# A new order for batches 0 to 2 of a two-stage attention and feed-forward kernel: transposes behind more matmuls, loads and transposes in other places

## The chip, the core and the metric

The kernel runs on one core of one Trainium2 chip. The metric is the device time of one execution in microseconds, lower is better. The core's engines are TensorE (PE, with its weight loads shown as PEld), VectorE (DVE), ScalarE (ACT), GpSimd (POOL) and SyncE (SP), which here only issues DMAs. Each engine works through its own list of instructions in order and waits for others by semaphores.

## The reference

The inputs are x (8 batches, 8 heads, 512 rows, 64 columns), a state of 32 rows per batch and head, and two weights of 512x2048 and 2048x512. For every batch and head the rows of x attend to the 32 state rows, and the state rows attend to x; both results are laid one under the other (544 rows a batch), heads side by side (512 columns), and go through a leaky feed-forward layer.

```python
scores = scale * np.matmul(x, state.transpose(0, 1, 3, 2))
a = softmax(scores)                      # max taken off, exp, divided by the sum + 1e-09
xread = np.matmul(a, state)
a2 = softmax(scale * np.matmul(state, x.transpose(0, 1, 3, 2)))
sread = np.matmul(a2, x)
attn = np.concatenate([xread, sread], axis=2)
h = attn_rows @ w_in                     # attn_rows: 4352 x 512
out = np.maximum(0.01 * h, h) @ w_out    # 4352 x 512, float32
```

## The kernel before

The 8 batches are worked one after the other, each through the same steps, and the steps of neighbouring batches are interleaved so that TensorE always has matmuls to do.

For a batch, x is loaded as float32 (`load_x`, tile `xl`, one buffer, 1 MB), cast to bfloat16 (`cast_x`, tile `xb`) and transposed by a DMA that SP issues (`a_xt_dma`, L207, tile `xT`). Batches 0 and 1 are transposed on TensorE instead (`turn` for batch 1, L1095: eight 128x128 transposes into `pxt`, evicted to `xT` by VectorE). `a_scores` (L223) makes the scores `sc` from `xT` and the state. VectorE and ScalarE make two softmaxes of it: over the state rows (`a_top`, `a_rows`, `a_less`, `a_exp`, `a_probs`, result `aT`), and over x's rows (`a_max2`, `a_exp2`, result `e2`). `a_a2t` (L330) transposes `e2` by a DMA into `a2T`, which `a_sread_rows` (L357, tile `psn`, called `rows` below) reads to make the second attention's product.

xread is never made by itself: `a_m` (L391, tile `pm`; `m_make`, `mk`) multiplies state and w_in into M, which is evicted to bfloat16 (`m_take`, `ev`), and `ff1` (L412, tile `ph`; `ff(j)`, `f.j`) multiplies M and `aT`, whose leaky ReLU (`relu`, `r.j`, L418) is the hidden tile `hT`. The second layer is made in two ways. Batch 0 uses plain matmuls: `piece(0, h0, i, jq)` (L697) adds up four (or with `part` two) of the 16 products of one output tile in PSUM (`py`, or `pyw`, the wide one), and `y_store` copies and stores the tile. Batches 1 to 7 use seven products instead of eight for a 2x2 block product, cut into units of two matmuls (L768, tile `yq`; `before.run(1)`, `u`); `sums` (L757) and `weights_sum` (L734) make the operands, `done` (`d.n`) saves or joins the products and issues the stores (L807).

Each engine's order is written out by hand: `tc.manual_schedule` keeps the order in which the program text emits the instructions for each of the five engines, so one line of the text can move an instruction on TensorE, another on VectorE, and a DMA in SP's list. Batch 1's part is a list of calls (from L1118 on). From batch 2 on `stretch(b, ...)` reads a string of short names; batch 2 has its own, FIRST, and batches 3 to 6 share ORDER. In these strings `l4` and `loads` are loads of x (`loads` of batch b + 3), `casts.h` its casts on GpSimd, `turn` the DMA transpose of batch b + 2, `a2t` the transpose of this batch's `e2`, `S` the next batch's scores, `st` the second group of the state, `sb` and `sn` operand sums of the earlier and the present batch. ORDER, used for batch 3, begins `sb.0.4 qs.0 u sb.1.4 rows S`: its `rows` for batch 3 reads the `a2T` of batches 1 and 2.

SP's order before, from batch 2 of x on, was: the state's transpose, both halves of batch 2's `xT`, the load of batch 3's x, `a2T` of batch 0, three stores of batch 0, half of the state's second group, `a2T` of batch 1, `xT` of batch 3, a store, the rest of the state, the load of batch 4's x, the state's second transpose, the load of batch 5's x, `a2T` of batch 2, `xT` of batch 4, two stores of batch 1.

Of the kernel before, what the change touches and what calls it, by code (L numbers as in the profile page):

```python
# [9 lines left out]
P = 128  # L10
# [20 lines left out]
def kernel(  # L31
# [255 lines left out]
    def a_rows(a):  # L287
        a.mb = block_rows(a.m1, NB)
# [402 lines left out]
    def piece(b, hT, i, jq, bank=None, copy=SCA, part=range(4)):  # L691
        if jq == 0:
            y = ys[b, i] = Y()
            y.py = psum.tile([P, DM], FP32, name="py", tag="py")[:] if bank is None else bank
        y = ys[b, i]
        for j in (4 * jq + v for v in part):
            nc.tensor.matmul(  # L697
                y.py, lhsT=hT[:, j, P * i:P * (i + 1)], rhs=w_out_bf[:, j, :],
                start=(j == 0), stop=(j == 15),
            )  # L700
        if jq == 3 and copy is not None:
            y_store(b, i, copy)
# [83 lines left out]
    class Batch:  # L786
# [44 lines left out]
        def done(self, n, bank, copy=SCA):  # L831
            f = self.f
            if n in (1, 6, 5, 7):
                f.save(n, bank, copy)
            if n == 2:
                f.join(self.yo(0)[:, :, :HC], bank, 1)
                if self.b == B - 1:
                    self.out(0, slice(0, HC))
            elif n == 7:
                nc.gpsimd.tensor_tensor(  # L840
                    out=self.yo(1)[:, :, HC:], in0=f.sv[7][:], in1=f.sv[5][:], op=ALU.add
                )
                if self.b == B - 1:
                    self.out(1, slice(HC, DM))
            elif n == 3:
                f.join(self.yo(0)[:, :, HC:], bank, 6)
                for i in range(2) if self.b in (2, 3, 4) else (None,):
                    self.out(0, slice(HC if self.b == B - 1 else 0, DM), i)
            elif n == 4:
                f.join(self.yo(1)[:, :, :HC], bank, 7)  # L850
                self.out(1)
# [247 lines left out]
    def cast_x1(u):  # L1099
        VEC(  # L1100
            a1.xb[:, :, NK * u:NK * (u + 1)].rearrange("p t h d -> p h t d"),
            x1[u][:].rearrange("p h (t d) -> p h t d", t=NT),
        )
# [10 lines left out]

    h1 = hpool.tile([P, 16, S], BF16, name="hT", tag="hT")
    before = Batch(1, h1)
    wide = psum.tile([P, 2, DM], FP32, name="pyw", tag="big", bufs=1)
    a_exp2(a0, 0)  # L1118
    piece(0, h0, 0, 0)
    load_state(0)  # L1120
    cast_x1(0)
    turn(0)
    cast_x1(1)
    piece(0, h0, 2, 0, bank=wide[:, 0])
    piece(0, h0, 1, 0)
    a_exp2(a0, 1)
    VEC(a1.xT[:, :, 0:2, :], pt[0][:])
    turn(1)
    VEC(a1.xT[:, :, 2:4, :], pt[1][:])
    piece(0, h0, 3, 0, bank=wide[:, 1])  # L1130
    m_make(a1, 1, "ph")
    open_xb(2)
    weights_open()
    a_scores(a1)
    m_take(a1, 1, 0, SCA)
    m_take(a1, 1, 1, VEC)
    a_top(a1)
    piece(0, h0, 0, 1, copy=None, part=(0, 1))
    piece(0, h0, 1, 1, copy=None, part=(0, 1))
    piece(0, h0, 2, 1, copy=None, part=(0, 1))  # L1140
    piece(0, h0, 1, 1, copy=None, part=(2, 3))
    m_make(a1, 2, "ph")
    m_take(a1, 2, 0, SCA)
    m_take(a1, 2, 1, SCA)
    weights_sum(2, 0, 4, nc.gpsimd)
    weights_sum(0, 0, 4, nc.gpsimd)
    state_t(0)
    piece(0, h0, 0, 1, copy=None, part=(2, 3))
    piece(0, h0, 2, 1, copy=None, part=(2, 3))
    piece(0, h0, 3, 1, copy=None, part=(0, 1))  # L1150
    m_make(a1, 3, "ph")
    piece(0, h0, 2, 2, copy=None, part=(0, 1))
    piece(0, h0, 1, 2, copy=None, part=(0, 1))
    a_rows(a1)
    a_less(a1)
    a_exp(a1)
    a_max2(a1)
    cast_x(2, 0, 4, SCA)
    cast_x(2, 4, 5, POO)
    cast_x(2, 5, 6, POO)  # L1160
    cast_x(2, 6, 7, POO)
    a_open(a2, 2)
    cast_x(2, 7, 8, POO)
    a_probs(a1, 0)
    piece(0, h0, 0, 2, copy=None, part=(0, 1))
    a_xt_dma(a2, slice(1, 2))
    piece(0, h0, 0, 2, copy=None, part=(2, 3))
    piece(0, h0, 3, 1, copy=None, part=(2, 3))
    piece(0, h0, 2, 2, copy=None, part=(2, 3))
    piece(0, h0, 3, 2, copy=None, part=(0, 1))  # L1170
    a_xt_dma(a2, slice(0, 1))
    a_exp2(a1, 0)
    a_probs(a1, 1)
    piece(0, h0, 1, 2, copy=None, part=(2, 3))
    piece(0, h0, 3, 2, copy=None, part=(2, 3))
    load_x(3, nc.sync)
    open_xb(3)
    piece(0, h0, 3, 3, copy=None, part=(0, 1))
# [27 lines left out]
    relu.pop(3)()
    y_store(0, 2, SCA)
    y_store(0, 3, SCA)
    piece(0, h0, 0, 3, copy=None, part=(0, 1))
# [21 lines left out]
    relu.pop(9)()
    y_store(0, 1, VEC)
    a_exp(a2)
    a_probs(a2, 0)
    before.run(1)
    a_probs2(a0)
# [16 lines left out]
    ff(14)
    relu.pop(14)()
    ff(15)
    relu.pop(15)()
# [326 lines left out]
```

## Time and profile before

| | |
|---|---|
| time before, median of 3 runs | 201.84 us (201.51 to 201.92) |
| profiled execution, its own time | 201.93 us |
| its span, first to last instruction | 200.2 us |
| mean granted TensorE clock | 1.000 |
| busy: PE, PEld | 193.9 us (97%), 136.5 us (68%) |
| busy: DVE, ACT, POOL | 164.7, 150.5, 62.2 us |
| DMA over the span | 28.02 MB, mean 140 GB/s |
| chain of work that ended last | PE 89%, DMA 6% |

The profile is one execution. Times in its timeline count from the first instruction; a row has a start, a length, the engine, the line of the kernel, the operation, what is written and read, and how many such instructions are merged in it. A bracket gives the idle time ahead of it and who ended it. SPq rows are DMAs that SP issues: their length is the time of the issue, not of the transfer. Matmul lengths overlap, since they are pipelined; the distance between two starts is what a matmul costs.

### The profile page before, as it was taken

What the parts mean: (1) busy time and instruction counts of PE and PEld (TensorE: products, weight loads), DVE (VectorE), ACT (ScalarE), POOL (GpSimd) and SP (SyncE); (2) the same over time, 40 slices, a digit from 0 to 9 for tenths busy, and PEclk for the clock granted to TensorE, in tenths of its full rate; (3) what the DMA queues carried; (4) which work ended last, traced back from release to release, by engine and by line L of the source; (5) the groups of instructions that cost most, each with busy time, mean ns of one, the idle gap of its engine ahead of it and who ended that gap; (6) DMA issues with size and microseconds to landing.
All of it is one profiled execution on the core that took longest, in us unless ns stands there. A gap on an engine that the chain in (4) does not pass through costs nothing.

```text
span 200.2 us, 5119 instructions
## 1 busy us (share of the span) xinstructions
PE 193.9 (97%) x2090; PEld 136.5 (68%) x2090; DVE 164.7 (82%) x283; ACT 150.5 (75%) x287; POOL 62.2 (31%) x90
## 2 busy tenths in 40 slices
PE   7999899999999999999999999999999999999992
PEld 2566544345677667776777777767777788799881
DVE  2676579799998989998999899999899977995622
ACT  3478728699778749996999679987999778767610
POOL 8483266591046013310422040400040024004350
PEclk9999999999999999999999999999999999999999
DMA  6999997999543994734393613080023402210035
GB/s 201 210 207 264 238 296 128 183 282 248 146 147 70 303 285 91 228 151 115 68 246 114 177 34 72 7 258 0 3 83 127 82 0 108 105 56 0 7 98 164
DMA packets 39992, 28.02 MB, mean 140 GB/s; under 512 B 25440, under 2 KB 36832, under 8 KB 39968
## 3 DMA queue, kind: packets, MB, share of 16 engines
q1 hardware_dynamic: 34176, 20.35, 38.1%
q0 software_dynamic: 4960, 6.55, 16.1%
q10 hardware_dynamic: 832, 0.79, 1.2%
q8 instruction: 16, 0.26, 0.6%
q14 instruction: 8, 0.07, 0.1%
HBM read 17.30 MB, written 8.91 MB: 131 GB/s over the span
## 4 chain that ended last, share of the span: by engine, by line
PE 89%; DMA 6%; DVE 1%; POOL 1%; ACT 0%; issue 0%
PE yq L768 43%; PE ph L412 18%; DMA x<-in_x_dram 6%; PE pm L391 4%; PE pyw L697 4%; PE py L697 3%; PE pf L490 3%; PE pl L658 3%; PE yu L768 3%; PE pspin L143 2%; PE pl L579 2%; PE psn L357 1%; PE sc L223 1%; PE phw L425 1%; PE pxt L1095 1%; PE yz L768 0%
## 5 line engine op out<-in xcount | busy, mean ns | idle before, releaser
L418 ACT ACTIVATE hT<-ph 128x512 bf16<-128x512 f32 x84 | 48.9, 609 | 12.3 <-PE ph L412 12.1
L768 PEld LDWEIGHTS <-su 128*128 128x128 bf16 x480 | 46.2, 98 | 12.6 <-ACT hT L418 0.4
L412 PE MATMUL ph<-aT,M 128*128 128x512 bf16 x168 | 47.6, 379 | 0.0
L768 PEld LDWEIGHTS <-hT 128*128 128x128 bf16 x336 | 32.3, 98 | 11.7 <-issue 2.5
L768 PE MATMUL yq<-tw_xf,su 128*128 128x256 bf16 x224 | 30.9, 273 | 0.0
L768 PE MATMUL yq<-w_out_bf,hT 128*128 128x256 bf16 x224 | 29.2, 273 | 0.0
L840 POOL TENSOR_TENSOR yo<-sv,sv 128x512 f32<-128x512 f32 x7 | 9.3, 1329 | 42.6 <-ACT e L311 38.2
L412 PEld LDWEIGHTS <-M 128*128 128x128 bf16 x168 | 16.0, 98 | 7.9 <-issue 1.9
L757 DVE TENSOR_TENSOR su<-hT 128x1024 bf16<-128x1024 bf16 x28 | 19.0, 682 | 2.7 <-ACT hT L418 2.7
L1288 ACT CAST M<-pm 128x512 bf16<-128x512 f32 x31 | 17.3, 599 | 1.4 <-PE pm L391 1.4
L114 POOL CAST xb<-xl 128x512 bf16<-128x512 f32 (+1 forms) x24 | 13.5, 604 | 12.6 <-DMA xl<-in_x_dram 12.6
L777 ACT COPY sv<-yq 128x512 f32<-128x512 f32 x24 | 13.9, 585 | 4.1 <-PE yq L768 4.0
L768 PE MATMUL yq<-tw_x,su 128*128 128x256 bf16 x112 | 16.6, 273 | 0.0
L780 DVE TENSOR_TENSOR yo<-yq,sv 128x512 f32<-128x512 f32 x20 | 13.5, 676 | 2.2 <-PE yq L768 2.2
L768 PE MATMUL yq<-w_out_bf,su 128*128 128x256 bf16 x112 | 15.3, 273 | 0.0
L768 PE MATMUL yq<-tw_x,hT 128*128 128x256 bf16 x104 | 13.9, 273 | 0.0
L311 ACT ACTIVATE e<-sc,mcol 128x512 bf16<-128x512 f32 x16 | 11.1, 698 | 0.0
L670 ACT COPY ls<-pl 128x512 f32<-128x512 f32 x16 | 9.5, 591 | 1.6 <-PE pl L658 1.4
L697 PEld LDWEIGHTS <-hT 128*128 128x128 bf16 x64 | 5.8, 98 | 7.0 <-issue 1.1
L757 DVE TENSOR_TENSOR su<-su,hT 128x1024 bf16<-128x1024 bf16 x14 | 9.6, 687 | 0.2
L305 DVE TENSOR_REDUCE mcol<-sc 128x2 f32<-128x1024 f32 x8 | 9.7, 1215 | 0.0
L1302 POOL COPY after<-mrow 128x1 f32<-128x1 f32 x3 | 0.6, 187 | 28.9 <-DVE mrow L233 28.9
(193 smaller groups left out, 359.9 us busy)
## 6 DMA issues: line engine op xcount, KB each, us to landing
xl<-in_x_dram SPq DMA_DIRECT2D x5, 1024.0 KB, 6.4
out_dram<-yo SPq DMA_DIRECT2D x9, 512.0 KB, 2.9
out_dram<-yo SPq DMA_DIRECT2D x9, 256.0 KB, 2.7
w_in_bf<-in_moe_w_in_dram POOLq DMA_DIRECT2D x4, 512.0 KB, 8.0
w_out_bf<-in_moe_w_out_dram POOLq DMA_DIRECT2D x2, 512.0 KB, 13.5
x<-in_x_dram POOLq DMA_DIRECT2D x2, 512.0 KB, 12.1
w_out_bf<-in_moe_w_out_dram POOLq DMA_DIRECT2D x4, 256.0 KB, 12.6
xl<-in_x_dram POOLq DMA_DIRECT2D x2, 512.0 KB, 15.2
```

Source lines behind the costliest of these rows:

```text
L114: copy(xs[b][:, h0 // NK, :, h0 % NK:h0 % NK + h1 - h0].rearrange("p t h d -> p h t d"), xl[b][:, h0:h1].rearrange("p h (t d) -> p h t d", ...
L305: nc.vector.tensor_reduce(out=a.m2[:], in_=a.sc[:], axis=AX.X, op=ALU.max, negate=True)
L311: nc.scalar.activation(out=a.e2[:, g], in_=a.sc[:, g, :], func=AF.Exp, bias=a.m2[:, g:g + 1], accum_out=a.r2[:, g:g + 1],)
L412: nc.tensor.matmul(ph[:], lhsT=a.M[:, g, P * j:P * (j + 1)], rhs=a.aT[:, g, :], start=(g == 0), stop=(g == 1),)
L418: nc.scalar.activation(out=hT[:, j, :], in_=ph[:], func=AF.Prelu, scale=1.0 / SCALE, alpha=0.01)
L670: copy(self.sv[n], flat)
L697: nc.tensor.matmul(y.py, lhsT=hT[:, j, P * i:P * (i + 1)], rhs=w_out_bf[:, j, :], start=(j == 0), stop=(j == 15),)
L757: (eng or nc.vector).tensor_tensor(out=S[n][:, ms], in0=u[:, ms], in1=v[:, ms], op=op)
L768: nc.tensor.matmul(bank[:, i, :], lhsT=lhs[:, m, P * i:P * (i + 1)], rhs=rhs[:, m, :], start=(first and m == 0 and (i == 0 or of is not No ...
L777: copy(t[:], bank)
L780: nc.vector.tensor_tensor(out=dst, in0=bank, in1=self.sv[n][:], op=ALU.add)
L1288: copy(t.M[:, g, DM * c:DM * (c + 1)], src[g][:] if isinstance(src, list) else src[:, g, :])
```

## The change

Batch 1's two sets of TensorE transposes and the pieces of batch 0 around them stand in another order: two pieces go ahead of the first set instead of one. After that the order of all five engines is another one, up to the end of batch 2's stretch (the list of calls and FIRST); ORDER stays. On SP the load of batch 3's x now goes between the two halves of batch 2's `xT`; batch 1's `a2T` and the first half of the state's second group go ahead of batch 0's stores; batch 4's `xT` goes ahead of batch 1's two stores, and the load of batch 5's x and batch 2's `a2T` go behind them. Some casts, evictions and copies change their engine. Apart from this part, batch 4 stores its first half with one transfer of 512 KB instead of two of 256 KB. The matmuls are the same in number and shape.

```diff
@@ Batch.done @@
             elif n == 3:
                 f.join(self.yo(0)[:, :, HC:], bank, 6)
-                for i in range(2) if self.b in (2, 3, 4) else (None,):
+                for i in range(2) if self.b in (2, 3) else (None,):
                     self.out(0, slice(HC if self.b == B - 1 else 0, DM), i)
@@ batch 1 @@
-    wide = psum.tile([P, 2, DM], FP32, name="pyw", tag="big", bufs=1)
     a_exp2(a0, 0)
     piece(0, h0, 0, 0)
+    cast_x1(0)
     load_state(0)
-    cast_x1(0)
+    cast_x1(1)
+    wide = psum.tile([P, 2, DM], FP32, name="pyw", tag="big", bufs=1)
+    piece(0, h0, 1, 0)
     turn(0)
-    cast_x1(1)
     piece(0, h0, 2, 0, bank=wide[:, 0])
-    piece(0, h0, 1, 0)
-    a_exp2(a0, 1)
-    VEC(a1.xT[:, :, 0:2, :], pt[0][:])
     turn(1)
-    VEC(a1.xT[:, :, 2:4, :], pt[1][:])
-    piece(0, h0, 3, 0, bank=wide[:, 1])
-    m_make(a1, 1, "ph")
     open_xb(2)
     weights_open()
+    VEC(a1.xT[:, :, 0:2, :], pt[0][:])
+    weights_sum(0, 0, 4, nc.gpsimd)
+    piece(0, h0, 3, 0, bank=wide[:, 1])
+    VEC(a1.xT[:, :, 2:4, :], pt[1][:])
+    a_exp2(a0, 1)
+    weights_sum(2, 0, 4, nc.gpsimd)
+    m_make(a1, 1, "ph")
     a_scores(a1)
...
-    cast_x(2, 0, 4, SCA)
-    cast_x(2, 4, 5, POO)
-    cast_x(2, 5, 6, POO)
-    cast_x(2, 6, 7, POO)
-    a_open(a2, 2)
-    cast_x(2, 7, 8, POO)
-    a_probs(a1, 0)
-    piece(0, h0, 0, 2, copy=None, part=(0, 1))
-    a_xt_dma(a2, slice(1, 2))
-    piece(0, h0, 0, 2, copy=None, part=(2, 3))
...
-    a_xt_dma(a2, slice(0, 1))
-    a_exp2(a1, 0)
+    a_open(a2, 2)
+    a_max2(a1)
+    cast_x(2, 0, 2, POO)
+    a_probs(a1, 0)
     a_probs(a1, 1)
+    cast_x(2, 2, 4, POO)
+    m_take(a1, 3, 0, SCA)
+    cast_x(2, 4, 8, SCA)
     piece(0, h0, 1, 2, copy=None, part=(2, 3))
+    a_xt_dma(a2, slice(1, 2))
+    piece(0, h0, 0, 2, copy=None, part=(2, 3))
     piece(0, h0, 3, 2, copy=None, part=(2, 3))
     load_x(3, nc.sync)
     open_xb(3)
...
+    a_xt_dma(a2, slice(0, 1))
+    a_exp2(a1, 0)
     cast_x(3, 0, 2, POO)
     a_exp2(a1, 1)
-    m_take(a1, 3, 0, SCA)
+    a_a2t(a0)
+    load_state(1, range(0, 2))
+    a_a2t(a1)
+    m_make(a2, 0, "sc")
...
-    a_a2t(a0)
-    a_scores(a2)
+    relu.pop(3)()
+    a_top(a2)
+    y_store(0, 3, SCA)
...
     FIRST = (
-        "f.1 f.0 l4 sb.0.4 u u r.1 u r.0 u f.2 d.1.A sb.2.0 f.3 mk.3.big r.2 S d.2 u u u sb.1.4 "
-        "tp ev.3.0.A r.3 f.4 u rows sb.2.4 u rw sb.3.4 u u u casts.0 casts.2 st u u u casts.4 f.5 "
-        "u ls sb.3.0 u u x2 casts.6 loads a2t turn u u ev.3.1.A d.6.A r.4 r.5 u w3 f.6 u d.5.A "
-        "f.7 r.6 u r.7 u f.9 ex u rc f.8 u u u u r.8 u r.9 u f.11 u u d.7.A u u u f.10 u u p2.1 "
-        "d.3 r.11 e2.0 e2.1 r.10 u u u u mk.2.ph mk.0.big mk.1.sc u u ev.1.0.A ev.2.0.A ev.2.1.V "
-        "ev.0.0.A ml d.4 ev.0.1.A p2.2 u u f.12 f.13 u u u r.13 u u u r.12 sn.0.0 f.15 f.14 u u u "
-        "u u ev.1.1.A u r.14 u r.15 dn.1 p2.3 sn.1.0 sn.2.0 "
+        "l4 u f.0 u sb.0.4 sb.2.4 f.1 u u f.3 r.0 f.2 r.1 d.1.A sb.1.4 sb.2.0 p2.1 S mk.3.big r.3 "
+        "rows u u u casts.0 r.2 ev.3.0.A casts.2 d.2 sb.3.0 sb.3.4 f.5 tp u u casts.4 u u "
+        "ev.3.1.A f.6 r.5 u u st u u casts.6 u rw turn ls u u u d.6.A r.6 f.4 u u r.4 u x2 f.7 u "
+        "d.5.A r.7 f.9 u ex r.9 u u u u u f.8 e2.0 r.8 d.7.V u u u u u u u f.10 w3 u d.3 rc f.11 "
+        "e2.1 r.10 r.11 u u u u u u mk.2.ph sn.0.0 p2.2 mk.1.sc mk.0.big ev.2.0.A u ev.1.0.A "
+        "ev.2.1.A d.4 u f.12 u u u u u f.13 u u f.14 u r.12 sn.2.0 f.15 ev.0.0.A r.13 ml u u u "
+        "r.14 ev.1.1.A r.15 loads u u ev.0.1.V u dn.1 a2t p2.3 sn.1.0 "
     )
```

More of the change, by code (lines that the diff above doesn't have):

```diff
@@ L1130 @@
-    piece(0, h0, 3, 0, bank=wide[:, 1])
-    m_make(a1, 1, "ph")
     open_xb(2)
     weights_open()
+    VEC(a1.xT[:, :, 0:2, :], pt[0][:])
[5 more added lines that the diff above has]
+    m_make(a1, 1, "ph")
     a_scores(a1)
+    piece(0, h0, 2, 1, copy=None, part=(0, 1))
+    piece(0, h0, 0, 1, copy=None, part=(0, 1))
     m_take(a1, 1, 0, SCA)
-    m_take(a1, 1, 1, VEC)
@@ L1137 @@
-    a_top(a1)
-    piece(0, h0, 0, 1, copy=None, part=(0, 1))
+    piece(0, h0, 0, 1, copy=None, part=(2, 3))
+    m_make(a1, 2, "ph")
     piece(0, h0, 1, 1, copy=None, part=(0, 1))
-    piece(0, h0, 2, 1, copy=None, part=(0, 1))
-    piece(0, h0, 1, 1, copy=None, part=(2, 3))
-    m_make(a1, 2, "ph")
     m_take(a1, 2, 0, SCA)
     m_take(a1, 2, 1, SCA)
-    weights_sum(2, 0, 4, nc.gpsimd)
-    weights_sum(0, 0, 4, nc.gpsimd)
+    m_take(a1, 1, 1, VEC)
+    piece(0, h0, 2, 1, copy=None, part=(2, 3))
@@ L1147 @@
+    a_top(a1)
+    a_rows(a1)
+    piece(0, h0, 1, 1, copy=None, part=(2, 3))
     state_t(0)
-    piece(0, h0, 0, 1, copy=None, part=(2, 3))
-    piece(0, h0, 2, 1, copy=None, part=(2, 3))
+    m_make(a1, 3, "ph")
+    piece(0, h0, 0, 2, copy=None, part=(0, 1))
+    piece(0, h0, 2, 2, copy=None, part=(0, 1))
     piece(0, h0, 3, 1, copy=None, part=(0, 1))
[L1151 to L1154, printed above, removed]
     a_less(a1)
-    a_exp(a1)
@@ L1157 @@
-    a_max2(a1)
-    cast_x(2, 0, 4, SCA)
-    cast_x(2, 4, 5, POO)
-    cast_x(2, 5, 6, POO)
-    cast_x(2, 6, 7, POO)
-    a_open(a2, 2)
-    cast_x(2, 7, 8, POO)
-    a_probs(a1, 0)
-    piece(0, h0, 0, 2, copy=None, part=(0, 1))
-    a_xt_dma(a2, slice(1, 2))
-    piece(0, h0, 0, 2, copy=None, part=(2, 3))
     piece(0, h0, 3, 1, copy=None, part=(2, 3))
@@ L1170 @@
     piece(0, h0, 3, 2, copy=None, part=(0, 1))
-    a_xt_dma(a2, slice(0, 1))
-    a_exp2(a1, 0)
+    piece(0, h0, 1, 2, copy=None, part=(0, 1))
+    a_exp(a1)
+    a_open(a2, 2)
+    a_max2(a1)
+    cast_x(2, 0, 2, POO)
+    a_probs(a1, 0)
     a_probs(a1, 1)
+    cast_x(2, 2, 4, POO)
+    m_take(a1, 3, 0, SCA)
+    cast_x(2, 4, 8, SCA)
     piece(0, h0, 1, 2, copy=None, part=(2, 3))
+    a_xt_dma(a2, slice(1, 2))
+    piece(0, h0, 0, 2, copy=None, part=(2, 3))
     piece(0, h0, 3, 2, copy=None, part=(2, 3))
@@ L1177 @@
     open_xb(3)
+    piece(0, h0, 2, 3, copy=None, part=(0, 1))
     piece(0, h0, 3, 3, copy=None, part=(0, 1))
@@ L1181 @@
     weights_sum(3, 4, 8, nc.gpsimd)
+    weights_sum(1, 0, 4, nc.gpsimd)
     weights_sum(0, 4, 8, nc.gpsimd)
-    weights_sum(1, 0, 4, nc.gpsimd)
+    a_xt_dma(a2, slice(0, 1))
+    a_exp2(a1, 0)
     cast_x(3, 0, 2, POO)
     a_exp2(a1, 1)
-    m_take(a1, 3, 0, SCA)
+    a_a2t(a0)
+    load_state(1, range(0, 2))
+    a_a2t(a1)
+    m_make(a2, 0, "sc")
     cast_x(3, 2, 4, POO)
     cast_x(3, 4, 6, POO)
-    piece(0, h0, 2, 3, copy=None, part=(0, 1))
-    m_make(a2, 0, "sc")
     m_take(a1, 3, 1, SCA)
@@ L1193 @@
     ff(1)
-    m_take(a2, 0, 0, VEC)
+    piece(0, h0, 2, 3, copy=None, part=(2, 3))
+    m_take(a2, 0, 0, SCA)
+    m_take(a2, 0, 1, VEC)
+    ff(2)
+    ff(3)
+    piece(0, h0, 3, 3, copy=None, part=(2, 3))
     relu.pop(0)()
-    piece(0, h0, 3, 3, copy=None, part=(2, 3))
-    m_take(a2, 0, 1, VEC)
     relu.pop(1)()
-    ff(2)
-    piece(0, h0, 2, 3, copy=None, part=(2, 3))
-    ff(3)
+    a_scores(a2)
+    y_store(0, 2, VEC)
+    piece(0, h0, 0, 3, copy=None, part=(0, 1))
     relu.pop(2)()
-    a_a2t(a0)
-    a_scores(a2)
+    relu.pop(3)()
+    a_top(a2)
+    y_store(0, 3, SCA)
     cast_x(3, 6, 8, POO)
[L1206 to L1209, printed above, removed]
+    ff(4)
     piece(0, h0, 0, 3, copy=None, part=(2, 3))
-    a_top(a2)
+    ff(5)
+    a_rows(a2)
     a_open(att_of[3], 3)
-    a_rows(a2)
+    a_less(a2)
+    relu.pop(4)()
     y_store(0, 0, SCA)
-    ff(4)
-    a_less(a2)
-    ff(5)
+    relu.pop(5)()
     ff(6, "big")
-    load_state(1, range(0, 2))
-    relu.pop(4)()
-    relu.pop(5)()
     ff(8)
+    ff(9)
     piece(0, h0, 1, 3, copy=None, part=(0, 1))
-    ff(9)
-    a_a2t(a1)
+    relu.pop(6)()
     a_xt_dma(att_of[3])
+    relu.pop(9)()
+    piece(0, h0, 1, 3, copy=None, part=(2, 3))
+    y_store(0, 1, VEC)
     a_max2(a2)
-    relu.pop(6)()
-    piece(0, h0, 1, 3, copy=None, part=(2, 3))
+    before.run(1)
+    a_exp(a2)
     relu.pop(8)()
[L1231 to L1236, printed above, removed]
     ff(10, "big")
@@ L1239 @@
     ff(12)
+    before.run(1)
+    a_probs(a2, 0)
+    ff(13)
+    before.run(1)
     relu.pop(10)()
-    before.run(1)
-    ff(13)
     before.run(1)
@@ L1245 @@
     before.run(1)
-    load_state(1, range(2, 4))
-    before.f.sums(0, 0, 4)
+    ff(14)
+    ff(15)
+    a_probs2(a0)
     a_probs(a2, 1)
@@ L1252 @@
     a_exp2(a2, 1)
[L1253 to L1256, printed above, removed]
     before.run(1)
@@ L1259 @@
     before.run(1)
+    relu.pop(15)()
+    relu.pop(14)()
     before.run(1)
+    m_make(a2, 1, "big")
+    m_make(a2, 2, "sc")
     before.run(1)
-    m_make(a2, 2, "sc")
-    m_make(a2, 1, "big")
+    m_take(a2, 1, 0, VEC)
+    before.f.sums(0, 0, 4)
     m_take(a2, 2, 0, SCA)
-    m_take(a2, 1, 0, VEC)
+    load_state(1, range(2, 4))
     m_take(a2, 2, 1, SCA)
-    before.run(1)
+    m_take(a2, 1, 1, VEC)
     before.f.sums(1, 0, 4)
-    m_take(a2, 1, 1, VEC)
     def stretch(b, hT, before, now, order):
```

## The prediction

> **What bounds the kernel now.** I read the page first, then TensorE's own waits, then its busy time in the long middle stretch, and only then the queues around the change.
>
> ```profile
> span 200.2 us, 5119 instructions
> PE 193.9 (97%) x2090; PEld 136.5 (68%) x2090; DVE 164.7 (82%) x283; ACT 150.5 (75%) x287; POOL 62.2 (31%) x90
> ```
>
> The waits of TensorE (who waited for whom: us in total, times, longest):
>
> ```profile
> PE pspin L143 <- DVE warm L76: 1.2, 1, 1.2
> PE pxt L1095 <- DVE xb L1100: 0.8, 1, 0.8
> ```
>
> Busy time by engine from 23 to 195 us (columns: stretch, length, then PE, PEld, DVE, ACT, POOL, granted clock, DMA share, GB/s):
>
> ```profile
> 23.00:195.00 172.00, 172.00 (x1789) 123.36 (x1790) 150.34 (x250) 135.44 (x261) 48.83 (x55) 1.00 0.49 128
> ```
>
> TensorE bounds the kernel. From 23 us on it has no gap, and the clock is full. Its only wait inside the program is 0.8 us at batch 1's transposes, for a cast that waits for a DMA. So no order of work can win more than about that wait, unless it shortens TensorE's own instructions, of which there are as many and of the same shapes as before. In the other direction there is no cushion: whatever makes TensorE wait anywhere after 23 us is added to the end, microsecond for microsecond. The question is therefore which operand can come late in the new order.
>
> **Batch 1's transposes behind one more piece: a gain of 0.7 us.** The timeline around them:
>
> ```profile
> 21.11 1.03 PE L697 MATMUL py<-w_out_bf,hT 128*128 128x512 bf16 x4
> 22.16 0.69 DVE L1100 CAST xb<-x 128x1024 bf16<-128x1024 f32 x1 [1.33 <-DMA x<-in_x_dram]
> 22.92 0.62 PE L1095 MATMUL pxt<-ident,xb 128*128 128x128 bf16 x8 [0.78 <-DVE xb L1100]
> 23.37 1.03 PE L697 MATMUL pyw<-w_out_bf,hT 128*128 128x512 bf16 x4
> 23.59 0.69 DVE L1100 CAST xb<-x 128x1024 bf16<-128x1024 f32 x1 [0.73 <-DMA x<-in_x_dram]
> 24.24 1.03 PE L697 MATMUL py<-w_out_bf,hT 128*128 128x512 bf16 x4
> 25.10 0.61 PE L1095 MATMUL pxt<-ident,xb 128*128 128x128 bf16 x8
> 25.75 0.69 DVE L1129 COPY xT<-pxt 128x1024 bf16<-128x1024 bf16 x1 [0.86 <-PE pxt L1095]
> 26.50 0.41 PE L391 MATMUL pm<-w_in_bf,st 64*32 64x512 bf16 x8
> ```
>
> A piece of four matmuls moves the next start by 0.87 us (23.37 to 24.24), eight transposes by 0.45 (22.92 to 23.37). In the new order the second py piece follows the first, from 21.98 to 22.84, and the transposes start at 22.92, when their cast is done: the old wait is filled. The first pyw piece ends at 24.24. The second set of transposes needs the second cast, which still hangs on its DMA and ends at 24.28; with the 0.07 us that lay between cast and transposes above, it starts at 24.35, waits 0.11, and ends at 24.80. The last pyw piece ends at 25.67. The matmuls of pm need the second copy of xT, which starts 0.65 after the transposes and takes 0.69: 25.69, so pm starts near 25.75 instead of 26.50. That is 0.75 us; I take 0.7, with 0.5 to 0.8 as bounds, because ScalarE's evictions of ph follow TensorE more closely in the new order and changes between full and 32-column matmuls are grouped otherwise.
>
> **Batch 2's second transpose behind batch 3's load: a loss of 4.2 us.** The SP queue is where the order costs something. The old sequence there, with its neighbours:
>
> ```profile
> 32.34 1.43 POOL L114 CAST xb<-xl 128x256 bf16<-128x256 f32 x4 [0.52 <-DMA xl<-in_x_dram]
> 32.39 1.03 ACT L114 CAST xb<-xl 128x1024 bf16<-128x1024 f32 x1
> 33.80 2.61 SPq L207 DMA_TRANSPOSE xT<-xb  x2
> 36.51 0.52 SPq L108 DMA_DIRECT2D xl<-in_x_dram  x1
> 37.09 2.49 SPq L330 DMA_TRANSPOSE a2T<-e  x1
> 38.86 0.41 PE L223 MATMUL sc<-xT,st_t 64*32 64x512 bf16 x8
> ```
>
> What was issued from 36 to 38 us (name, KB, us from issue to landing):
>
> ```profile
> xl<-in_x_dram SPq DMA_DIRECT2D x1, 1024.0 KB, 6.8
> xT<-xb SPq DMA_TRANSPOSE x1, 3.2
> a2T<-e SPq DMA_TRANSPOSE x1, 7.1
> ```
>
> And from 62 to 63.5 us:
>
> ```profile
> xl<-in_x_dram SPq DMA_DIRECT2D x1, 1024.0 KB, 6.0
> ...
> a2T<-e SPq DMA_TRANSPOSE x1, 6.3
> ```
>
> And a transpose of the same size with no load ahead of it, from 131 to 133 us:
>
> ```profile
> a2T<-e SPq DMA_TRANSPOSE x1, 3.7
> ```
>
> The reader is to see this: a transpose alone lands 3.2 to 3.7 us after its issue, but issued some 0.6 us behind the 1 MB load it lands 6.3 or 7.1 us after, both times 0.9 us behind the load itself (36.51 + 6.8 = 43.3 against 37.09 + 7.1 = 44.2; 62.30 + 6.0 = 68.3 against 62.91 + 6.3 = 69.2). What SP issues is served in its order of issue. The Trainium skill (DMA: Bandwidth & Descriptors, "Queues, rings and completion order") says that all DMAs of one issuing engine share one ring on each DMA engine, consumed in ring order; the rows agree, and it speaks against this change.
>
> Before, both halves of batch 2's xT stood ahead of batch 3's load. Now the load stands between them. The half that ScalarE casts goes first: its data are there at 32.3 (GpSimd's cast starts then), the cast takes 1.03, so the transpose is issued near 33.4 and holds SP for 1.3 (half of 2.61). The load goes out at 34.7, the other half 0.58 later, at 35.3. With the load's 6.8 us and 0.9 behind it, xT is whole at 42.4. Ahead of batch 2's scores stand the same matmuls in both orders, so TensorE wants them at 38.86 - 0.7 = 38.2, and it waits 4.2 us. Everything later on TensorE is queued behind that wait. All loads of `xl`, by line (the longest is one of two that GpSimd issued at the start):
>
> ```profile
> DMA to landing us min/median/max: 5.5/6.6/15.7
> ```
>
> With 5.5 the wait is 2.9. I take 6.8, since it is the same load in the same place, behind the same transposes; 0.3 more if SP issues it later: 2.9 to 4.5.
>
> **Batch 2's a2 transpose at the end of its stretch: a loss of 3.3 us.** a2T of batch 2 was issued at 62.91 and read by the psn matmuls of batch 3's stretch (`rows`) at 71.50. Now `a2t` is the last SP entry of FIRST, behind `loads` (batch 5's 1 MB), which is behind the store of `d.4`.
>
> ```profile
> 62.30 0.52 SPq L108 DMA_DIRECT2D xl<-in_x_dram  x1
> 62.91 1.53 SPq L330 DMA_TRANSPOSE a2T<-e  x1
> 66.62 1.03 PE L412 MATMUL ph<-aT,M 128*128 128x512 bf16 x4
> 67.39 0.68 DVE L780 TENSOR_TENSOR yo<-yq,sv 128x512 f32<-128x512 f32 x1
> 69.03 1.01 SPq L807 DMA_DIRECT2D out_dram<-yo  x2
> 69.66 1.91 PE L768 MATMUL yq<-w_out_bf,hT 128*128 128x256 bf16 x16
> 71.50 0.70 PE L357 MATMUL psn<-xb,a2T 128*32 128x64 bf16 x64
> ```
>
> Count from the matmul that finishes the sum for `d.4`. TensorE's way to psn: 16 units of two matmuls (15 in FIRST, one in ORDER); eight units took 71.50 - 69.66 = 1.84 with a change to 32-column matmuls at their end, so 0.22 each: 3.5; four `f`, each half of 67.48 - 66.62, that is 0.43: 1.7; batch 1's half of psn, 0.3. Together 5.5 us. SP's way: 0.2 until the last matmul has drained (four matmuls' row is 1.03 long, their steps 0.87), the join 0.68 and its signal, 0.95; half of the two stores' 1.01, the load 0.6 (62.30 to 62.91), so a2T is issued at 2.1 and lands 6.3 later, at 8.4: 2.9 us late. The load also has a 512 KB store ahead of it, so it will rather take the median's 6.6 than the 6.0 on which the 6.3 stands: I add 0.4 and take 3.3. With 5.5 for the load it is 2.4, with 7.1 for a2T 3.7.
>
> **What costs nothing.** The other moves are on VectorE, ScalarE and GpSimd, which the 172 us row shows busy for 150, 135 and 49; while TensorE stands still for 4 us they catch up, so their new order hides behind the first loss. Without that cover I price it at 0.2 to 0.3 (the first half's transpose landing, 35.3 + 3.2 = 38.5, against 38.2). State and output transfers that trade places on SP have readers far away. Batch 4's store goes out as one 512 KB transfer instead of two of 256: the next thing on SP is a transpose at 131.59,
>
> ```profile
> 129.18 2.31 SPq L807 DMA_DIRECT2D out_dram<-yo  x3
> 131.59 1.49 SPq L330 DMA_TRANSPOSE a2T<-e  x1
> ```
>
> whose reader, by the chain, is
>
> ```profile
> 155.93 0.62 PE psn L357 x64
> ```
>
> 24 us later. A microsecond more or less there meets no one.
>
> **Sum.** -0.7 + 4.2 + 3.3 = +6.8 us. The profiled execution took 201.93 us (span 200.2), the median of the runs 201.84; on the median that is 208.6 us. With all bounds: +4.5 to +7.7, 206.3 to 209.5.
>
> **Rivals.** *The transposes are not held by the load (not slower).* If a transpose could pass the load, xT would be whole 3.2 after 35.3, 0.3 late, and a2T would land 3.7 after 2.1, at 5.8 against 5.5, 0.3 late: -0.7 + 0.6 gives 201.7, or 201.4 if neither is late. It decides where a transpose's landing comes less than about 3.5 us after issue. For it: each carries its own signal. Against it: both times that the trace has a load just ahead. The same section of the skill warns that completion is not in order per issuing engine, which would be this case; the two rows here do not bear that out. Chance 0.08.
>
> *Only the first wait stands.* If VectorE joins `d.4` earlier against TensorE, or the load finds the queue empty and a2T follows quickly, the second wait goes: 201.84 + 3.5 = 205.3. The count leaves 2.4 at the least, so 0.06. *Only the second stands*, if the first half's cast comes so early that the load is over in time: it would need 2.9 us: 201.84 - 0.7 + 0.3 + 3.3 = 204.7. Chance 0.06.
>
> *The wait drops the clock.* At the kernel's start the same matmul shape ran slower:
>
> ```profile
> 1.18 3.17 PE L143 MATMUL pspin<-idle 128*128 128x512 bf16 x7 [1.18 <-DVE warm L76]
> 4.74 1.27 PE L143 MATMUL pspin<-idle 128*128 128x512 bf16 x3
> ```
>
> Six steps in 3.17 less one matmul's 0.6, 0.43 a step against 0.22 later, until about 5.6 us: 4.4 us at half pace. If the 4.2 us wait brings that state back, some 4.4 us of matmuls run at half pace, +2.2: 210.8. The 0.8 us wait did not: the transposes after it ran at full pace. The Trainium skill (TensorE: Matmul & The Clock Gate, Part 1) lets the clock fall after an idle window of about 3.4 us in free-running windows, so a 4.2 us wait would seldom hold a whole one; no row here shows a drop after a wait. Chance 0.12.
>
> **How the numbers follow.** Forecast with both waits and a full clock 0.66, clock drop 0.12, first alone 0.06, second alone 0.06, neither 0.08, 0.02 for what I have not seen. The range 204.7 to 210.8 takes in the forecast with its bounds, the first alone, and half of the second alone and of the clock drop: 0.81. The forecast's own range is 206.3 to 209.5. About 0.2%, 0.4 us, is what a measurement of this kernel can tell from no change. Only the case with neither wait can end near or below it: 201.4 to 201.7 is mostly within it, so 0.03 faster, 0.05 the same, 0.92 slower.
>
> **What would show it.** Right: TensorE's waits name xT at the scores of batch 2 near 38 us (4 us) and a2T at psn near 75 us (3 us), the 0.8 us at pxt shrinks to 0.1 and 0.1; a transpose lands about 0.9 us behind the load just ahead of it. Wrong: TensorE has no gap after 25 us, or the transposes land 3 to 4 us after issue with the load still under way, or a third wait of VectorE's or ScalarE's making stands at the top of the list.

## The result and the profile after

The changed kernel takes 214.43 us (median of 6 runs, 213.6 to 214.75), the kernel before 201.81 us beside it (6 runs, 201.51 to 202.49): 6.16% slower, ratio 1.0616 [1.0590, 1.0642]. The prediction was 208.6 us with a range to 210.8, so the sign and both places are right and the size is not: the loss is 12.6 us where 6.8 was forecast. The profiled execution took 214.48 us with a span of 212.7; before it was 201.93 and 200.2, so 12.55 us are to be found.

The page's first lines, busy time by engine, and the granted clock over the span in 40 slices of 5.3 us:

```profile
span 212.7 us, 5118 instructions
...
PE 198.4 (93%) x2090; PEld 137.7 (65%) x2090; DVE 165.9 (78%) x284; ACT 150.3 (71%) x286; POOL 62.2 (29%) x88
...
PE   7999999199999954999999999999999999999993
...
PEclk9999999969999995799999999999999999999999
```

TensorE has the same 2090 matmuls and yet is busy for 198.4 us instead of 193.9. So 4.5 us of the loss are not waiting at all, but matmuls that took longer, and the clock row says where most of it lies: in the slices behind the two holes in the PE row. TensorE's waits (who waited for whom: us in total, times, longest):

```profile
PE psn L357 <- DMA a2T<-e: 5.0, 1, 5.0
PE sc L223 <- DMA xT<-xb: 4.3, 1, 4.3
PE pspin L143 <- DVE warm L76: 1.2, 1, 1.2
```

The two waits forecast are there, at the matmuls named, and the wait at `pxt` is gone. The timeline of TensorE, from the transposes to the second wait:

```profile
21.08 1.89 PE L697 MATMUL py<-w_out_bf,hT 128*128 128x512 bf16 x8
25.65 0.41 PE L391 MATMUL pm<-w_in_bf,st 64*32 64x512 bf16 x8
42.61 0.41 PE L223 MATMUL sc<-xT,st_t 64*32 64x512 bf16 x8 [4.35 <-DMA xT<-xb]
42.96 1.03 PE L697 MATMUL py<-w_out_bf,hT 128*128 128x512 bf16 x2
46.34 1.03 PE L425 MATMUL phw<-aT,M 128*128 128x512 bf16 x4
77.18 0.42 PE L357 MATMUL psn<-xb,a2T 128*32 128x64 bf16 x32
82.59 0.62 PE L357 MATMUL psn<-xb,a2T 128*32 128x64 bf16 x32 [4.99 <-DMA a2T<-e]
84.95 2.34 PE L768 MATMUL yq<-tw_xf,su 128*128 128x256 bf16 x10
88.06 0.82 PE L768 MATMUL yq<-tw_xf,su 128*128 128x256 bf16 x6
```

`pm` starts at 25.65 instead of 26.50. Behind the first wait two full matmuls show 1.03 us, at 46.34 again four do: half pace for 3.4 us. Behind the second wait ten matmuls of 256 columns show 2.34 us, at 88.06 six show 0.82. The same stretches by engine and clock (columns: stretch, length, then busy us and instructions of PE, PEld, DVE, ACT, POOL, granted clock, DMA share, GB/s):

```profile
39.50:42.90 3.40, 0.29 (x8) 0.11 (x8) 0.00 (x0) 0.11 (x1) 3.40 (x3) 1.00 1.35 199
42.90:46.30 3.40, 3.40 (x16) 1.19 (x9) 3.14 (x3) 1.16 (x2) 2.07 (x4) 0.50 0.85 217
77.10:80.40 3.30, 0.49 (x34) 0.30 (x32) 1.31 (x4) 0.59 (x1) 0.00 (x0) 1.00 1.11 272
80.40:83.80 3.40, 1.21 (x48) 0.60 (x48) 0.42 (x1) 0.00 (x0) 0.00 (x0) 0.51 0.84 92
83.80:87.20 3.40, 3.40 (x21) 1.92 (x14) 3.37 (x5) 0.60 (x1) 2.05 (x5) 0.50 0.00 0
87.30:91.00 3.70, 3.70 (x30) 2.73 (x28) 2.40 (x6) 3.09 (x6) 0.32 (x1) 1.00 0.66 123
```

In its records the clock is halved from 42.92 to 46.34 and from 80.47 to 87.30. TensorE works at half pace from 42.92 to 46.34 (3.41 us, 1.7 lost) and from 82.59 to 87.30 (4.71 us, 2.35 lost). The account: -0.8 at the transposes, 4.35 + 1.7 at the first place, 4.99 + 2.35 at the second, together 12.6 of the 12.55 us; an experiment below adds a term of -0.5 at the very end, so about 0.5 us is left over. It lies around the first wait: from `pm` to the first `psn` row it is 45.00 us before (26.50 to 71.50) and 51.53 after (25.65 to 77.18), and the wait and its half clock are 6.05 of these 6.53. It comes with the wait and not with the new order as such: the kernel e11 below, with the same matmuls in the same order and without the wait, takes 44.97 us there (25.55 to 70.52). What it is stays open.

The queue at the two places, SP's issues first, then the landings (KB, us from issue to landing) of what was issued from 35 to 36 us and from 73.6 to 74.5 us, where the load, still being issued, is listed too:

```profile
34.67 0.45 SPq L108 DMA_DIRECT2D xl<-in_x_dram  x1
35.17 2.05 SPq L207 DMA_TRANSPOSE xT<-xb  x1
37.26 3.33 SPq L330 DMA_TRANSPOSE a2T<-e  x1
73.26 0.39 SPq L108 DMA_DIRECT2D xl<-in_x_dram  x1
73.75 6.29 SPq L330 DMA_TRANSPOSE a2T<-e  x2
```

```profile
xl<-in_x_dram SPq DMA_DIRECT2D x1, 1024.0 KB, 6.1
xT<-xb SPq DMA_TRANSPOSE x1, 7.4
```

```profile
xl<-in_x_dram SPq DMA_DIRECT2D x1, 1024.0 KB, 7.0
a2T<-e SPq DMA_TRANSPOSE x1, 8.8
```

xT lands at 35.17 + 7.4 = 42.57, 1.8 behind its load (34.67 + 6.1 = 40.77); a2T lands at 82.55, 2.3 behind its load (80.26). Before, the two transposes that stood right behind a load had landed 0.9 behind it.

### The profile page after: what moved, and what is told of

It is laid out like the page before. It is cut to its first block, busy times and chain, and to the rows that moved or that the text cites. A ratio compares the mean times of both kernels' runs of the same rounds, so it can differ in the third digit from the quotient of the medians.

```text
span 212.7 us, 5118 instructions
## 1 busy us (share of the span) xinstructions
PE 198.4 (93%) x2090; PEld 137.7 (65%) x2090; DVE 165.9 (78%) x284; ACT 150.3 (71%) x286; POOL 62.2 (29%) x88
## 4 chain that ended last, share of the span: by engine, by line
PE 77%; DMA 18%; SPq 1%; DVE 1%; ACT 0%; issue 0%; POOL 0%
PE yq L768 40%; PE ph L412 17%; DMA xl<-in_x_dram 7%; DMA a2T<-e 4%; DMA w_in_bf<-in_moe_w_in_dram 4%; DMA xT<-xb 3%; PE pf L490 3%; PE pl L658 3%; PE yu L768 3%; PE pm L391 3%; PE pspin L143 2%; PE pl L579 2%; PE py L697 1%; PE sc L223 1%; PE psn L357 1%; PE phw L425 1%
## 5 line engine op out<-in xcount | busy, mean ns | idle before, releaser
L768 PEld LDWEIGHTS <-su 128*128 128x128 bf16 x480 | 46.8, 99 | 12.7 <-issue 0.6
L412 PE MATMUL ph<-aT,M 128*128 128x512 bf16 x168 | 49.4, 389 | 0.0
L768 PE MATMUL yq<-tw_xf,su 128*128 128x256 bf16 x224 | 31.9, 279 | 0.0
L768 PE MATMUL yq<-w_out_bf,hT 128*128 128x256 bf16 x224 | 29.7, 273 | 0.0
L114 POOL CAST xb<-xl 128x512 bf16<-128x512 f32 x22 | 13.0, 628 | 14.2 <-DMA xl<-in_x_dram 14.2
L777 ACT COPY sv<-yq 128x512 f32<-128x512 f32 x23 | 13.3, 584 | 3.1 <-PE yq L768 3.0
L233 DVE TRANSPOSE_TENSOR_REDUCE mrow<-sc 128x32 f32<-128x1024 f32 x7 | 8.7, 1244 | 4.3 <-PE sc L223 4.3
```

The lines of the kernel that those rows point to most:

```text
L114: copy(xs[b][:, h0 // NK, :, h0 % NK:h0 % NK + h1 - h0].rearrange("p t h d -> p h t d"), xl[b][:, h0:h1].rearrange("p h (t d) -> p h t d", ...
L233: nc.vector.tensor_reduce(out=m1[:], in_=flat.rearrange("p (c j) -> p c j", j=NS), axis=AX.X, op=ALU.max, apply_transpose=True,)
L412: nc.tensor.matmul(ph[:], lhsT=a.M[:, g, P * j:P * (j + 1)], rhs=a.aT[:, g, :], start=(g == 0), stop=(g == 1),)
L768: nc.tensor.matmul(bank[:, i, :], lhsT=lhs[:, m, P * i:P * (i + 1)], rhs=rhs[:, m, :], start=(first and m == 0 and (i == 0 or of is not No ...
L777: copy(t[:], bank)
```

## The experiments

**One place mended (e1), the other (e2), both (e3).** In the changed kernel, both xT halves go ahead of the load, or a2T of batch 2 goes out right behind batch 4's xT, ahead of the two stores and the load.

```diff
+    a_xt_dma(a2, slice(0, 1))        # e1, e3
     load_x(3, nc.sync)
...
-    a_xt_dma(a2, slice(0, 1))
-  "... rw turn ls u u u ..."         # e2, e3: in FIRST
+  "... rw turn a2t ls u u u ..."
-  "... u dn.1 a2t p2.3 sn.1.0 "
+  "... u dn.1 p2.3 sn.1.0 "
```

> The changed kernel, but both halves of batch 2's xT go out ahead of batch 3's load on SP. If SP's order makes the wait at batch 2's scores, that wait (4.35 us) and the 3.4 us at half clock behind it (1.7 us) go: 214.4 - 6.05 = 208.4 us, and the second half lands 3 to 4 us after its issue. If the DMA engines are merely too busy there, whatever the order, the wait stays above 3 us and the time within 1 us of 214.4.

> The changed kernel, but batch 2's a2T goes out right behind batch 4's xT, ahead of batch 1's stores and of batch 5's load. By SP's order the wait at psn (4.99 us) and the half clock behind it (4.7 us at half, 2.35 us) go: 214.4 - 7.3 = 207.1 us. By mere DMA load: within 1 us of 214.4.

> The changed kernel with both of these. If the two DMA orders are the whole loss, 214.4 - 13.4 = 201.0 us, 0.4% faster than before, with no TensorE wait over 0.3 us after 25 us and a clock of 1.00. If the new order of the other engines costs something of its own that the two waits hid, waits of VectorE's or ScalarE's making appear and it is slower than 201.8 us.

Measured: e1 207.78 us, ratio to before 1.0275 [1.0231, 1.0319]; e2 207.91 us, 1.0294 [1.0264, 1.0325]; e3 200.87 us, 0.9970 [0.9950, 0.9989]. TensorE's wait on a DMA in each of the three:

```profile
PE psn L357 <- DMA a2T<-e: 4.7, 1, 4.7
```

```profile
PE sc L223 <- DMA xT<-xb: 4.2, 1, 4.2
```

```profile
PE sc L223 <- DMA xT<-xb: 0.7, 1, 0.7
```

Each mended place takes its own wait away and leaves the other: the first is worth 214.43 - 207.78 = 6.65 us, the second 6.52. Nothing of the 12.6 us is left when both are mended, so no third place carries a loss of any size. The 0.7 us in e3 is neither of the two waits:

```profile
45.37 3.62 SPq L207 DMA_TRANSPOSE xT<-xb  x1
52.51 0.41 PE L223 MATMUL sc<-xT,st_t 64*32 64x512 bf16 x8 [0.69 <-DMA xT<-xb]
```

These are batch 3's scores, and they wait for batch 3's whole xT, which landed 7.1 us after its issue at 45.37. In e1 it was issued at 45.33, landed after 6.0, and nothing waited. The profiled execution of e3 took 201.82 us, well above the median of 200.87. In e1 one of four runs took 205.5 us with a mean clock of 0.992, the others 207.4 to 208.35 with 0.983: by the mean clock, the same wait cost one half-clock stretch of 3.4 us there and two here.

**The first place alone, in the kernel before (e6).** The load is put between the two halves, and nothing else is changed.

```diff
-    a_xt_dma(a2, slice(0, 1))
     load_x(3, nc.sync)
+    a_xt_dma(a2, slice(0, 1))
```

> The kernel before with one move: batch 2's second transpose goes behind batch 3's load on SP. If this place alone makes the first wait, xT lands 1 to 2 us behind the load, TensorE waits some 4 us at batch 2's scores and runs 3.4 to 6.8 us at half clock: 201.8 + 4.1 + 1.7 to 2.5 = 207.6 to 208.4 us. If the wait needs the rest of the new order, it stays under 203 us.

Measured: 209.0 us, 1.0336 [1.0301, 1.0371], with a wait of 4.4 us at the scores. The half lands 7.5 us after its issue, at 43.18, 1.8 behind its load, the same as in the changed kernel. Two lines of SP's order are enough for half of the loss.

**a2T away from the transpose that follows it (e8).** In the changed kernel, batch 3's a2T, the next DMA of SP behind batch 2's, is moved on behind batch 5's xT.

```diff
         def turn():
             ...
+            if b == 3:
+                a_a2t(a)
-    a2t=lambda: a_a2t(a),
+    a2t=lambda: b != 3 and a_a2t(a),
```

> The changed kernel, but batch 3's a2T goes behind batch 5's xT on SP, so that no transpose follows directly on batch 2's a2T. If the transpose that follows is why a2T landed 2.3 us behind its load instead of 0.9, it lands about 1 us behind it and the wait at psn is 3.5 us instead of 5.0: 214.4 - 1.4 = 213.0 us, or less by another half microsecond of half clock. If not, the landing stays 2.3 us behind the load and the time at 214.4 us.

Measured: 213.04 us, 1.0556 [1.0535, 1.0577]; the wait at `psn` is 3.5 us. The load, and a2T issued 0.48 us behind it (74.08 and 74.56):

```profile
xl<-in_x_dram SPq DMA_DIRECT2D x1, 1024.0 KB, 6.7
```

```profile
a2T<-e SPq DMA_TRANSPOSE x1, 7.3
```

Without batch 3's a2T behind it, it lands 1.1 us behind its load; with it, 2.3 (in e1 as well: load 67.02 + 6.7, a2T 67.50 + 8.5). That is most of the part of the second wait that the prediction did not have. But it is not so that any transpose right behind does this. In the kernel before, batch 2's a2T, issued at 62.91, had batch 4's xT right behind it and still landed 0.9 behind its load:

```profile
64.53 4.41 SPq L207 DMA_TRANSPOSE xT<-xb  x1
```

Nor is it always the one behind: batch 3's a2T, right behind batch 5's load in e2, e3, e11 and e12 and with nothing issued for 9 us after it, landed 1.0 to 1.1 behind the load in three of the traces and 2.4 behind it in e11. Why is open.

**The two loads on GpSimd's queue (e5).** In the changed kernel:

```diff
-    load_x(3, nc.sync)
+    load_x(3, nc.gpsimd)
...
-                load_x(b + 3, nc.sync)
+                load_x(b + 3, nc.gpsimd if b == 2 else nc.sync)
```

> The changed kernel, all orders kept, but the loads of batch 3's and batch 5's x are issued by GpSimd, on its own queue, at the same places in the text. If what holds the transposes is their place behind the load in SP's queue, xT and a2T land some 3 to 5 us after issue though the same megabyte moves at the same time, and both waits shrink to under 1.5 us: about 202 to 204 us. If the bandwidth of the DMA engines is the cause, they land 6 us or more after issue as before, both waits stay near 4 us and the time stays above 210 us.

Measured: 210.33 us, 1.0422 [1.0401, 1.0443]: neither theory. TensorE's waits, and the landings of what was issued from 71.3 to 72.5 us and from 75 to 76.5:

```profile
PE sc L223 <- DMA xT<-xb: 5.5, 1, 5.5
...
PE psn L357 <- DMA a2T<-e: 1.0, 1, 1.0
```

```profile
xl<-in_x_dram POOLq DMA_DIRECT2D x1, 1024.0 KB, 6.6
```

```profile
a2T<-e SPq DMA_TRANSPOSE x1, 5.3
```

GpSimd issues the first load at 33.80 and it takes 8.3 us to land, at 42.1; the scores start at 43.79, when the half has landed, 1.6 behind the load although it is on another queue. The second place shows less. The load goes out earlier, at 71.68, and lands 6.6 later at 78.3; a2T, issued at 75.29, lands 5.3 later at 80.6, 2.3 behind, but here one of batch 1's stores of 512 KB stands right ahead of it in SP's own queue. So "served in its order of issue" says too little: at the first place a 1 MB load in flight on the other queue, too, held the transpose until behind its own end. The Trainium skill (DMA: Bandwidth & Descriptors, "Queues, rings and completion order") has each DMA engine go round its queues packet by packet. From 38 to 40 us the trace agrees: 114 packets of the load's queue and 106 of SP's. But the load's are of 4 KB and SP's of less than 512 bytes, so that 0.47 MB of the load moved and 0.03 MB of what SP had issued: equal turns by packet do not let a transpose get ahead. From 36 to 38 us SP's queue moved only 16 packets against 70; why is open.

**Is the half clock the idle time's doing (e4)?** Matmuls of zeros fill the waits of the changed kernel, and only add work: 17 of 512 columns ahead of batch 2's scores, 75 of 128 columns ahead of batch 2's part of `psn`.

```diff
+        for _ in range(17 if a.b == 2 else 0):
+            nc.tensor.matmul(sc[:, 0, :], lhsT=idle[:, :P], rhs=idle[:], start=True, stop=True)
...
+            for _ in range(75 if u == 1 and a.b == 2 else 0):
+                nc.tensor.matmul(ps[...], lhsT=idle[:, :P], rhs=idle[:, :P], start=True, stop=True)
```

> The changed kernel with 17 matmuls of zeros (3.7 us) ahead of batch 2's scores and 75 small ones (4.2 us) ahead of batch 2's half of psn: TensorE is busy while it would wait, and the xT and a2T that it waits for land as before. If the half clock comes from the idle time, the granted clock stays full and only the two waits are lost: 214.4 - 1.7 - 2.35 = 210.4 us. If the half clock comes from something else, or the slow matmuls are slow for the DMAs beside them, it stays at 214.4 us, with the same rows at half pace.

Measured: 210.5 us, 1.0431 [1.0416, 1.0447]. The transposes are as late as before (xT 7.3 us, a2T 8.8), and what TensorE still waits for them is

```profile
PE psn L364 <- DMA a2T<-e: 0.7, 1, 0.7
PE sc L225 <- DMA xT<-xb: 0.6, 1, 0.6
```

The clock stays full to the end, and the kernel is 3.9 us faster with 92 useless matmuls more. That is the half clock's share of the loss, 1.7 + 2.35 in the account above.

**How much idle time does it take (e12)?** The kernel e2, which has the wait on xT alone, with 12 matmuls of zeros in it.

```diff
+        for _ in range(12 if a.b == 2 else 0):
+            nc.tensor.matmul(sc[:, 0, :], lhsT=idle[:, :P], rhs=idle[:], start=True, stop=True)
```

> The changed kernel with a2T issued early, so that only the wait on xT of about 4.2 us is left, and 12 matmuls of zeros (512 columns each, about 2.6 us together) ahead of batch 2's scores: they only add work inside the wait, and leave some 1.6 us of it idle. Without them it took 207.9 us, of which by its clock row 2.6 us are 6.8 us at half clock. If the clock falls only where most of a window of 3.4 us is idle, it stays full and the time is about 205.3 us; if 1.6 us of idle time is enough to lose it, 207 to 208 us.

Measured: 205.43 us, 1.0184 [1.0169, 1.0199], full clock, with 1.8 us of wait left. The emptiest stretch of 3.4 us in step with the clock (counted on from 6.37 us, where its full speed begins), and the one that follows:

```profile
40.50:43.90 3.40, 1.65 (x15) 0.60 (x13) 0.69 (x1) 0.00 (x0) 3.40 (x4) 1.00 1.21 157
43.90:47.30 3.40, 3.40 (x17) 1.57 (x16) 3.03 (x3) 2.99 (x6) 1.32 (x3) 1.00 1.01 266
```

TensorE was busy for 1.65 us of it, and the clock stayed. In e8 1.19 us were too few:

```profile
37.30:40.70 3.40, 1.19 (x6) 0.29 (x3) 0.70 (x2) 1.78 (x4) 3.40 (x2) 1.00 1.11 311
40.70:44.10 3.40, 1.29 (x10) 0.41 (x11) 0.59 (x1) 0.00 (x0) 3.40 (x4) 0.50 0.95 156
```

**Batch 4's single store (e7), and batch 3's in its place (e13), in the kernel before.**

```diff
-                for i in range(2) if self.b in (2, 3, 4) else (None,):
+                for i in range(2) if self.b in (2, 3) else (None,):     # e7
+                for i in range(2) if self.b in (2, 4) else (None,):     # e13
```

> The kernel before with batch 4's first half stored in one transfer. Priced at nothing: 201.8 us, within 0.2%. If one larger store delays what is behind it on SP, up to 0.5 us slower.

> The kernel before with batch 3's first half, and not batch 4's, stored in one transfer. With batch 4's in one transfer the kernel before took 201.4 us, 0.24% less, and all of it lies behind the last matmul: SP's last instructions wait for the semaphores of the transfers one after the other, some 0.06 us each, and with one transfer fewer the last store falls on the last of them, not on the second. If that is the cause, one transfer fewer anywhere ahead does the same, and this takes 201.4 us too; if it is the store of batch 4 itself (its place, its size), it takes 201.8 us.

Measured: e7 201.43 us, 0.9976 [0.9967, 0.9986]; e13 201.33 us, 0.9981 [0.9972, 0.9990]. Neither was priced in the prediction, and both are the same 0.2%. It lies behind the last matmul. From that matmul's start to SP's last instruction it is 196.14 to 200.09 us before, 3.95, and 196.04 to 199.53 in e7 and 196.26 to 199.74 in e13, 3.49 and 3.48; in the changed kernel, which has one transfer fewer as well, 209.11 to 212.60, 3.49. SP's last instructions in the trace wait for the transfers' semaphores in a fixed order (start, and the number of the first semaphore):

```
before:  198.83 S100   198.89 S102   198.96 S103  ...  199.20 S117   199.26 S118
e7:      197.27 S100   197.33 S102   ...  198.28 S116   198.34 S117   198.71 S118
```

Before, the last store signals S100, and seven more waits of 0.06 us each come behind that one. With one transfer fewer, of batch 4 or of batch 3, the transfers get other semaphores, the last store signals S118, and the other waits are over by then. So it is the count of transfers and not the store of batch 4.

**Batch 1's transposes behind one more piece, in the kernel before (e10).**

```diff
+    piece(0, h0, 1, 0)
     turn(0)
...
-    piece(0, h0, 1, 0)
```

> The kernel before with one edit: batch 1's projection piece of the other half is put ahead of the turn, so that its transposes of batch 1 stand behind one more piece; the stores and the order of SP stay as before. If the first term of the prediction (-0.7) is right, the wait of 0.7 us on batch 1's xT goes and the time is about 201.1 us (ratio 0.9965); if that term was an accident of the trace after, where other things moved too, it stays at 201.8 us.

Measured: 201.42 us, 0.9988 [0.9978, 0.9998]: a gain of 0.25 us, a third of what was expected. The wait at `pxt` is gone:

```profile
21.54 1.89 PE L697 MATMUL py<-w_out_bf,hT 128*128 128x512 bf16 x7
23.27 0.61 PE L1095 MATMUL pxt<-ident,xb 128*128 128x128 bf16 x8
```

What it had been worth varies, as two kernels show that have the old order there, e6 and e7 (first `py`, then the transposes):

```profile
21.14 1.03 PE L697 MATMUL py<-w_out_bf,hT 128*128 128x512 bf16 x4
22.87 0.62 PE L1095 MATMUL pxt<-ident,xb 128*128 128x128 bf16 x8 [0.71 <-DVE xb L1100]
```

```profile
21.63 1.03 PE L697 MATMUL py<-w_out_bf,hT 128*128 128x512 bf16 x4
22.82 0.62 PE L1095 MATMUL pxt<-ident,xb 128*128 128x128 bf16 x8 [0.17 <-DVE xb L1100]
```

The cast sets the transposes' start near 22.9 (22.8 to 23.0 in the four traces with the old order), whenever TensorE comes. In the 14 profiled executions TensorE comes to `py` at 21.04 to 21.27 where the full clock begins by 6.0 us, and at 21.45 to 21.71 where it begins at 6.4 to 7.2 us; the wait takes up the difference. Removing it gains 0.2 to 0.8 us, by the execution. The trace of before, and that of after, were early ones.

**Both mended, and the xT half whose casts end first issued first (e11).** In e3:

```diff
+    a_xt_dma(a2, slice(0, 1))
     a_xt_dma(a2, slice(1, 2))
...
-    a_xt_dma(a2, slice(0, 1))
```

> The changed kernel with batch 3's a2T issued early and both xT halves ahead of batch 3's load, and in addition the two halves issued in the other order, the half whose casts are done first going first. In the same kernel with the halves in their old order PE still waits 0.7 us on the second xT half. If that wait is only the order of the two halves on SP, it shrinks to 0.2 to 0.3 us and the time is about 200.4 us; if it is the transfer itself, 200.9 us.

Measured: 200.62 us, 0.9957 [0.9943, 0.9971], the lowest median of all, though its interval overlaps that of e3. The wait of 0.7 us at the scores is gone, but that does not show that the order of the two halves made it. It stood in e3 at batch 3's scores, not at batch 2's, which waited for neither half. In e11 batch 3's xT, in the same place on SP, lands 5.9 us after its issue at 44.91 and is in time, as in e1 with the old order of the halves. So what the order of the halves is worth is not shown.

## Why the prediction was right or wrong

*Transposes behind one more piece, -0.7:* right in the profiled execution (0.85 at `pm`), but the term hung on how early TensorE came in one execution; by e10 it is worth 0.25 in the median.

*Batch 2's second xT half behind the load, +4.2:* right, 4.35 here, 4.2 in e2, 4.4 in e6. Two errors cancelled: the load landed in 6.1 us, not 6.8, and the half 1.8 behind it, not 0.9.

*a2T at the end of the stretch, +3.3 with 3.7 as the upper bound:* mis-sized, 4.99. The step that failed is "both times 0.9 us behind the load itself": here a2T landed 2.3 behind, and the load took 7.0 us, not 6.6. The 0.9 came from two rows with other neighbours on SP, stores behind the one and batch 4's xT behind the other. Here batch 3's a2T was behind it; e8 takes that away and gets 1.1 and a wait of 3.5. Why this neighbour matters and the xT did not is open.

*"What SP issues is served in its order of issue":* true for the two orders compared, but e5 shows that a load on the other queue held the transpose at the first place just as long.

*Batch 4's store at nothing:* wrong by 0.5 us. The prediction looked for a reader of the data and not at the waits that end the program.

*The clock, +2.2 with a chance of 0.12:* this is the step that failed most, 4.05 us. The prediction saw the right mechanism and nearly the right price for one drop (2.2 us; measured 1.7 and 2.35), then gave it little chance, because the Trainium skill (TensorE: Matmul & The Clock Gate, Part 1) lets the clock fall after at least one idle window of about 3.4 us in free-running windows, and it read that as a window without any matmul. The trace agrees on the length, 3.41 us, and on free running: the clock's changes at 5.38, 42.92, 46.34, 80.47 and 87.30 us lie whole multiples of 3.41 apart. It does not agree on "idle" as read: stretches with 0.29 and 0.49 us of matmuls dropped it, in e8 one with 1.19; 1.65 in e12 and 2.16 in the changed kernel (36.1 to 39.5) kept it. A wait of 4.2 us leaves at most 3.41 x 2 - 4.2 = 2.6 us for two neighbouring windows, so one of them has 1.3 or less whatever the phase. By these rows such a wait nearly always costs the clock, and the chance should have been near 1, for each of the two waits. The runs say the same: all 6 of the changed kernel show a mean clock of 0.976, and all 16 of e1, e2, e5, e6 and e8, which keep a wait of 3.5 us or more, 0.992 or less, where the kernel before shows 0.996 to 1.000.

Both kinds of error add up: 4.05 for the clock, 1.7 for the second wait, 0.15 for the first, against -0.1 and -0.5 for the first term and the store, give 5.3 of the 5.8 us that were missed; the rest is the half microsecond around the first wait, whose cause is open.

## What to carry to other kernels

Price a wait of TensorE as the wait plus what the clock takes behind it: here waits of 3.5 to 5.5 us cost 1.5 to 3.1 us more (half the matmul time at half clock behind each), and filling part of one with useless matmuls took that away. Put a transpose that is needed soon ahead of a large load and not behind it, on whichever queue the load is, and look at its neighbours on the queue too. A term that rests on a wait near the start of one execution is only as good as that execution.

## What the runs showed of the hardware that was not expected

The clock seems to come back by the same kind of count. At half clock a stretch of 3.4 us with 2.69 us of matmuls was followed by another half one (e6), one with 3.06 us by a full one (e8):

```profile
42.60:46.00 3.40, 2.69 (x14) 0.89 (x15) 1.96 (x2) 0.20 (x1) 3.18 (x5) 0.50 0.65 192
46.00:49.40 3.40, 3.40 (x10) 1.16 (x9) 2.90 (x3) 1.77 (x4) 0.00 (x0) 0.50 0.33 105
```

```profile
81.60:85.00 3.40, 3.06 (x54) 1.41 (x55) 2.24 (x4) 0.46 (x1) 0.50 (x2) 0.51 0.00 0
85.00:88.40 3.40, 3.40 (x27) 2.47 (x26) 3.40 (x7) 2.14 (x5) 1.97 (x4) 0.99 0.06 11
```

Counted as work at full pace, 2.69 and 3.06 us at half clock are 0.40 and 0.45 of a stretch. Of the full-clock ones 0.35 (1.19 us) lost the clock and 0.49 (1.65 us) kept it. One limit between 0.40 and 0.45 fits all of them, but nothing here tested it by itself.

The end of this program has a price that depends on how many DMAs came ahead: 0.5 us of serial waits of 0.06 us each, or nothing, by where the last store's semaphore stands in their order.
